# Splitting the output stores of an attention and feed-forward kernel into 32-row pieces

## The chip, the cores and the metric

One core of one Trainium2 chip. The metric is the device time of one execution in microseconds (us); the kernel before takes 597.29 us, the median of three runs (596.9 to 598.46).

## What is computed

Chunked local attention with a few memory keys, and a feed-forward layer on its result. Four sequences of 768 positions, 8 heads of 64; a chunk of 32 queries sees 8 memory keys and a window of 16 + 32 + 8 keys. The heads are put side by side, which gives 3072 tokens of 512 numbers; these go through 512 to 2048 to 512 with a squared, clipped gate. All of it is f32.

```python
for c in range(nc):                       # chunks of 32 queries, 24 a sequence
    k_full = concatenate([mem_k, k_ctx], axis=2)
    v_full = concatenate([mem_v, v_ctx], axis=2)
    scores = scale * matmul(q_c, k_full.transpose(0, 1, 3, 2))
    scores = scores - max(scores, axis=-1, keepdims=True)
    a = exp(scores)
    a = a / (sum(a, axis=-1, keepdims=True) + 1e-09)
    out[:, :, c_start:c_end] = matmul(a, v_full)
x = attn_out.transpose(0, 2, 1, 3).reshape(B * S, H * D)
h = x @ w_in
g = where(h >= 1, h, where(h <= -1, 0, (h + 1) ** 2 / 4))
return g @ w_out
```

## The kernel before, in words

The 3072 tokens are six blocks (`blk` 0 to 5) of 512 tokens, and each block is four token tiles `t` of 128 rows. A tile of the result is 128 rows of 512 f32, 2 KB a row, 256 KB in all. TensorE adds it up in PSUM over 16 slices `fc` of the hidden layer; then DVE or ACT copies it into an SBUF tile `ob`, and a DMA takes it to `out`.

Blocks 0 and 1 go by a hand-written order of steps (`FIRST`, lines 32 to 46). The rest, the end of block 1 and blocks 2 to 5, goes through a planner (class `Plan`, lines 65 to 174). Each step is told to it by `add(engine, took, emit, reads, writes)`: `took` is what the step is supposed to cost in us, and `reads` and `writes` give its dependencies. `due_times` works back from TensorE's steps to the time by which each step is due. `run` then goes through the steps in simulated time, takes for each engine the one that is ready and due first, and so fixes the order of each engine's queue. A step on another engine is ready only some time after the one it needs has ended: 2.0 us where that one is a DMA step on SP (`AFTER`, line 67). What is issued on an engine is kept in that order, and all instructions are recorded on line 191, the line of the helper that does this. Engines wait in order: what stands behind a waiting instruction waits too.

All DMAs are issued from SP. Blocks 2 and 3 make one pair and blocks 4 and 5 another: the first of a pair is worked out straight, the second from differences, with weights that come back from DRAM in units through seven slots (`SLOTS`, line 1129; `load_unit`, tiles named `u_w`, `u_xth`, `u_xtl` in the trace). A slot's next unit is loaded when TensorE has left the slot.

`store(blk, t, key, src)` (lines 1022 to 1053) copies one finished tile to `ob` and adds the DMA step `put`. For `t` = 3 DVE copies the left half and ACT the right. For `blk` under `first` = 2 `put` is one DMA of 128 contiguous rows. From block 2 on the rows of a pair of tiles alternate in DRAM by 32, so that `put` writes four groups of 32 rows, 64 rows apart, in one DMA, whose DRAM side has the shape 4 x 32 x 512:

```python
rows = out[r0 : r0 + HT, :].rearrange("(n b q) d -> b n q d", b=2, q=CHUNK)
sp.dma_start(rows[b], dst())
```

Where `ob` lies decides who waits for a store. For blocks 2 and 4 it is in the tag `f` (two buffers, used later by `tf` and `uc`). For blocks 3 and 5 all four tiles are one SBUF tile under the tag `w_14`. In `tee_ops(1)` (line 1204), between blocks 3 and 4 on one side and 5 on the other, ACT writes the operand `b22` to that same tag (`high("b22", b(1), x32)`, line 1266; `b<-x` in the trace). So this ACT step waits until the four stores of block 3 have landed. ACT's next steps there are the copy `c` (line 1354), which reads a PSUM bank that TensorE then adds on to, and the cast `gh`.

The DMA step that loads a unit is told to the planner as 2.1 or 2.8 us (line 1162), a store as 0.8 us.

Of the kernel before, what the change touches and what calls it, by code (L numbers as in the profile page):

```python
# [17 lines left out]
CHUNK, LEFT, RIGHT = 32, 16, 8  # L18
TB = 512
NCH = TB // CHUNK  # L20
NT = TB // P
# [43 lines left out]
class Plan:  # L65
# [7 lines left out]
    def place(self, key, *tags, bufs=1):  # L73

        waits = self.waits.setdefault(key, set())
        for tag in tags:
            line = self.tenants.setdefault(tag, [])
            if line:
                waits.update(self.touched.get(line[-1], [])[:1])
            if len(line) >= bufs:  # L80
                waits.update(self.touched.get(line[-bufs], ()))
            line.append(key)

    def add(self, engine, took, emit, reads=(), writes=(), soon=False):

        deps = set()
        for keys, writing in ((reads, False), (writes, True)):
            for key in keys:
                base, part = key if isinstance(key, Part) else (key, None)
                deps |= self.waits.get(base, set())  # L90
                state = self.state.setdefault(base, {})
                for name, (writer, readers) in state.items():
                    if part is None or name is None or name == part:
                        deps.update(writer)
                        if writing:
                            deps.update(readers)
        op = Op(engine, took, emit, deps, len(self.ops))
        op.soon = soon
        for x in deps:
            x.then.append(op)  # L100
        for keys, writing in ((reads, False), (writes, True)):
            for key in keys:
                base, part = key if isinstance(key, Part) else (key, None)
                state = self.state[base]
                if writing:
                    if part is None:
                        state.clear()
                    state[part] = ([op], [])
                else:
                    state.setdefault(part, ([], []))[1].append(op)  # L110
                self.touched.setdefault(base, []).append(op)
        self.ops.append(op)
        return op
# [83 lines left out]
def attn_ffn_kernel(ctx: ExitStack, tc: tile.TileContext, first_qk, first_v, qk, vw, w, out):  # L197
    nc = tc.nc
    engines = (nc.tensor, nc.scalar, nc.vector, nc.gpsimd, nc.sync)
    pe, act, dve, pool, sp = (InOrder(tc, e) for e in engines)  # L200
# [7 lines left out]
    NB = qk.shape[0] + 1  # L208
# [20 lines left out]
    HT = TB // 2  # L229
# [77 lines left out]
    first = 2  # L307
# [404 lines left out]
    a, b = n_first["J9"], len(tokens) - 1  # L712
    put = []
# [16 lines left out]
    add, place = plan.add, plan.place  # L730
# [3 lines left out]
    def tile_of(key, make):  # L734
        if key not in tiles:
            tiles[key] = make()
        return tiles[key]
# [11 lines left out]
    def on(engine, took, reads, writes, call, *args, **kwargs):  # L749

        def emit():
            call(*(a() if callable(a) else a for a in args), **kwargs)

        add(engine, took, emit, reads, writes)
# [241 lines left out]
    def out_job(name, outs, fc, w, reads, blk=None):  # L996

        gh, gl = (part_tile(name, which) for which in ("gh", "gl"))
        kinds = [(gh, 0, ("gh", name)), (gh, 1, ("gh", name)), (gl, 0, ("gl", name))]

        def terms(which):
            def get():
                for t, i in which:
                    g, part, _ = kinds[i]
                    yield (
                        outs[t][1](), g()[:, t * P : (t + 1) * P], w(part), fc == 0 and i == 0,
                        fc == NFC - 1 and i == 2,
                    )

            return get  # L1010

        if fc < NFC - 1:
            for i in range(3):
                mm(terms([(t, i) for t in range(NT)]), NT, [kinds[i][2], *reads], [k for k, _ in outs])
                yield
            return
        for t in range(NT):
            mm(terms([(t, i) for i in range(3)]), 3, [("gh", name), ("gl", name), *reads], [outs[t][0]])
            store(blk, t, *outs[t])
            yield  # L1020

    def store(blk, t, key, src):

        apart = blk in (3, NB - 1)
        ob = ("ob", blk, 0 if apart else t // 2)
        if t == 0 or t == 2 and not apart:
            place(ob, *(("w_14",) if apart else ("f",)), bufs=1 if apart else 2)

        def dst():
            if apart:  # L1030
                return tile_of(ob, lambda: const.tile([P, NT, DM], F32, name="ob4", tag="w_14"))[:, t]
            return tile_of(ob, lambda: apool.tile([P, 2, DM], F32, name="ob", tag="f", bufs=2))[:, t % 2]

        if t == NT - 1:
            on("dve", 0.4, [key], [Part(ob, (t, 0))], dve.tensor_copy, lambda: dst()[:, 0:HD], lambda: src()[:, 0:HD])
            on("act", 0.35, [key], [Part(ob, (t, 1))], act.copy, lambda: dst()[:, HD:DM], lambda: src()[:, HD:DM])
        elif t % 2:
            on("act", 0.6, [key], [Part(ob, (t, 0))], act.copy, dst, src)
        else:
            on("dve", 0.7, [key], [Part(ob, (t, 0))], dve.tensor_copy, dst, src)  # L1040

        def put():
            if blk < first:
                r0 = blk * TB + t * P
                sp.dma_start(out[r0 : r0 + P, :], dst())
            else:
                half, b = divmod(t, 2)
                r0 = blk * TB + half * HT
                rows = out[r0 : r0 + HT, :].rearrange("(n b q) d -> b n q d", b=2, q=CHUNK)
                sp.dma_start(rows[b], dst())  # L1050

        add("sp", 0.8, put, [Part(ob, (t, 0)), *([Part(ob, (t, 1))] if t == NT - 1 else [])], [])

    jobs = []

# [28 lines left out]
    for name in ("D2", "D3"):  # L1084
        n = pair_of[name]
# [204 lines left out]
    for u in range(2):  # L1290
# [90 lines left out]
        a, b = hb  # L1381
# [175 lines left out]
```

## Time and profile before

| | us |
|---|---|
| median of three runs | 597.29 |
| the profiled execution's own time | 596.54 |
| its span, from the first to the last instruction | 594.7 |
| TensorE (PE) busy | 559.4 |
| VectorE (DVE) busy | 392.1 |
| ScalarE (ACT) busy | 319.5 |
| GpSimd (POOL) busy | 56.0 |
| DMA queue of SP, share of 16 engines' span | 59.7% |

The profile shows one execution, in us from its first instruction. A line of a timeline has start, duration, engine, operation, output<-input and the number of instructions merged in it; a bracket gives the idle time of the engine before it and what ended that. "SPq" is SP's queue: the duration of a DMA there is the time it takes SP to issue it, not to move the data. A tile's name stands for all its buffers.

### The profile page before, as it was taken

Reading aid. Unit: us, or ns where it says so; the run is one execution under the profiler, and the core shown is the slowest. Engines: PE = TensorE matmul, PEld = TensorE weight load, DVE = VectorE, ACT = ScalarE, POOL = GpSimd, SP = SyncE. Lnnn points to the kernel's source line nnn. Section 1 sums busy time; section 2 is a strip of 40 time slices with the busy share of each in tenths; the row PEclk is TensorE's granted clock in tenths of the full one; section 3 lists DMA queues with packets and bytes.
Section 4 is the critical chain, followed back from the end, with each engine's and each line's share of the span. In section 5 each row is a group of like instructions: output and inputs, shape, how many; then the busy total and the mean of one; then the engine's idle time right before and its main releaser. Section 6 shows DMA issues by size and latency. Waiting matters only on the chain.

```text
span 594.7 us, 12467 instructions
## 1 busy us (share of the span) xinstructions
PE 559.4 (94%) x5268; PEld 457.2 (77%) x5268; DVE 392.1 (66%) x556; ACT 319.5 (54%) x524; POOL 56.0 (9%) x55
## 2 busy tenths in 40 slices
PE   5899999999999999999999999899599999999990
PEld 3788887888887888887878778688488887888880
DVE  4899899737877858688687686658123566664220
ACT  3987666544766667764655664466243544453210
POOL 1010000007679200000000000000000000000000
PEclk9999999999999999999999999999899999999997
DMA  8999969536481846852664976644533546477102
GB/s 318 422 418 424 407 200 393 216 139 253 165 297 75 316 151 241 304 208 93 240 239 142 352 284 255 229 179 141 208 125 128 192 161 224 166 253 265 50 0 71
DMA packets 35352, 132.93 MB, mean 224 GB/s; under 512 B 3296, under 2 KB 5344, under 8 KB 28896
## 3 DMA queue, kind: packets, MB, share of 16 engines
q1 hardware_dynamic: 35296, 132.13, 59.7%
q8 instruction: 41, 0.67, 0.4%
q14 instruction: 15, 0.12, 0.1%
HBM read 102.76 MB, written 29.36 MB: 222 GB/s over the span
## 4 chain that ended last, share of the span: by engine, by line
PE 79%; DVE 6%; ACT 6%; DMA 4%; issue 2%; SPq 1%; ACTq 0%; DVEq 0%
PE ps_h L191 33%; PE a L191 31%; PE ps_o L191 11%; PE ps_x L191 3%; DMA out_dram<-ob 2%; DMA w<-in_w_dram 2%; PE ps_s L191 1%; DVE f L191 1%; ACT gw L191 1%; DVE gl L191 1%; ACT pt L191 1%; ACT pr L191 1%; ACT wr L191 1%; DVE pr L191 1%; DVE wr L191 1%
## 5 line engine op out<-in xcount | busy, mean ns | idle before, releaser
L191 PE MATMUL ps_h<-xth,wr 128*128 128x512 f32 (+1 forms) x384 | 84.2, 357 | 1.3 <-ACT gw L191 0.6
L191 PEld LDWEIGHTS ps_h<-xth,wr 128*128 128x128 f32 x384 | 64.6, 188 | 13.6 <-DVE gw L191 1.1
L191 PE MATMUL ps_o<-wr,gh 128*128 128x512 f32 x256 | 66.0, 393 | 0.2 <-ACT gh L191 0.2
L191 ACT ACTIVATE gw<-gw 128x512 f32<-128x512 f32 (+1 forms) x104 | 62.3, 599 | 3.2
L191 DVE TENSOR_TENSOR gl<-gw,gh 128x512 fp32r<-128x512 f32 (+1 forms) x72 | 51.4, 719 | 9.5 <-ACT gh L191 8.0
L191 ACT CAST gh<-gw 128x512 fp32r<-128x512 f32 (+1 forms) x72 | 40.8, 570 | 29.0 <-DVE gw L191 22.5
L191 PEld LDWEIGHTS ps_o<-wr,gh 128*128 128x128 f32 x256 | 47.0, 188 | 10.0 <-ACT gh L191 0.6
L191 PE MATMUL a<-u_w,gh 128*128 128x512 f32 x180 | 54.1, 391 | 0.0
L191 DVE TENSOR_TENSOR gl<-gq,gh 128x512 fp32r<-128x512 f32 x32 | 21.9, 688 | 40.7 <-PE ps_h L191 24.4
L191 PE MATMUL ps_h<-xtl,wr 128*128 128x512 f32 (+1 forms) x192 | 46.0, 354 | 0.0
L191 PE MATMUL ps_h<-u_w,gh 128*128 128x512 f32 x132 | 41.1, 391 | 2.2 <-issue 2.2
L191 ACT CAST gh<-gq 128x512 fp32r<-128x512 f32 x32 | 19.7, 622 | 41.2 <-PE ps_h L191 25.9
L191 ACT ACTIVATE gw<-gq 128x512 f32<-128x512 f32 x32 | 20.2, 632 | 38.6 <-DVE gq L191 35.7
L191 PEld LDWEIGHTS a<-u_w,gh 128*128 128x128 f32 x180 | 33.6, 188 | 9.5 <-issue 2.4
L191 DVE SCALAR_TENSOR_TENSOR gw<-ps_h,gw 128x512 f32<-128x512 f32 (+1 forms) x48 | 28.4, 593 | 18.7 <-ACT gw L191 18.6
L191 PEld LDWEIGHTS ps_h<-xtl,wr 128*128 128x128 f32 x192 | 32.9, 189 | 5.2
L191 ACT ACTIVATE gw<-ps_h 128x512 f32<-128x512 f32 (+1 forms) x48 | 25.0, 521 | 22.0 <-PE ps_h L191 15.4
L191 PE MATMUL ps_h<-t,u_w 128*128 128x512 f32 x144 | 36.4, 395 | 0.0
L191 PE MATMUL ps_o<-wr,gl 128*128 128x512 f32 x128 | 36.2, 391 | 0.0
L191 PE MATMUL a<-t,u_w 128*128 128x512 f32 x138 | 35.0, 396 | 0.0
L191 PEld LDWEIGHTS ps_h<-t,u_w 128*128 128x128 f32 x144 | 26.6, 188 | 7.0 <-DVE gq L191 1.5
L191 PEld LDWEIGHTS a<-t,u_w 128*128 128x128 f32 x138 | 25.4, 188 | 7.1 <-DVE gq L191 1.8
(145 smaller groups left out, 1024.1 us busy)
## 6 DMA issues: line engine op xcount, KB each, us to landing
u_w<-d_out SPq DMA_DIRECT2D x39, 512.0 KB, 7.1
qk<-in_qk_dram SPq DMA_DIRECT2D x10, 1536.0 KB, 14.2
w<-in_w_dram SPq DMA_DIRECT2D x14, 1024.0 KB, 17.8
u_w<-d_sum SPq DMA_DIRECT2D x12, 1024.0 KB
v<-in_vw_dram SPq DMA_DIRECT2D x10, 1024.0 KB
d_out<-wr SPq DMA_DIRECT2D x16, 512.0 KB, 9.0
out_dram<-ob SPq DMA_DIRECT2D x24, 256.0 KB, 2.0
u_xtl<-d_out SPq DMA_DIRECT2D x9, 512.0 KB, 5.0
```

The costliest lines, as they stand in the source:

```text
L191: return self.tc.keep_in_program_order(getattr(self.engine, name)(*args, **kwargs))
```

## The change

`put` no longer writes a tile of blocks 2 to 5 in one DMA but in four of 32 contiguous rows (64 KB) each, so that 16 DMAs become 64. Those of the very last tile (block 5, `t` = 3) are issued in turn from SP and from ACT, two each. The cost of the step as told to the planner rises from 0.8 to 1.9 us for these blocks. Blocks 0 and 1 stay as they are.

```diff
             else:
                 half, b = divmod(t, 2)
                 r0 = blk * TB + half * HT
-                rows = out[r0 : r0 + HT, :].rearrange("(n b q) d -> b n q d", b=2, q=CHUNK)
-                sp.dma_start(rows[b], dst())
-
-        add("sp", 0.8, put, [Part(ob, (t, 0)), *([Part(ob, (t, 1))] if t == NT - 1 else [])], [])
+                for n in range(4):
+                    r = r0 + (2 * n + b) * CHUNK
+                    by = act if t == NT - 1 and blk == NB - 1 and n % 2 else sp
+                    by.dma_start(out[r : r + CHUNK, :], dst()[n * CHUNK : (n + 1) * CHUNK])
+
+        add("sp", 0.8 if blk < first else 1.9, put, [Part(ob, (t, 0)), *([Part(ob, (t, 1))] if t == NT - 1 else [])], [])
```

## Rows read from the trace of the kernel before

**Rows 1.** The page: the span in 40 slices, each 14.87 us; busy tenths.

```profile
PE   5899999999999999999999999899599999999990
PEclk9999999999999999999999999999899999999997
```

**Rows 2.** Waits of TensorE: us in total, times, longest.

```profile
PE a L191 <- ACT c L191: 7.2, 1, 7.2
...
PE ps_h L191 <- issue: 2.2, 1, 2.2
```

**Rows 3.** SP's waits, whole span: us in total, times, longest.

```profile
SPq L191 <- DMA w<-in_w_dram: 26.6, 16, 2.2
...
SPq L1553 <- DMA out_dram<-ob: 10.7, 1, 10.7
```

**Rows 4.** The chain of waits around 410 to 434: start, us, what.

```profile
410.12 2.73 PE a L191 x12
...
414.31 13.57 DMA out_dram<-ob
...
427.98 1.04 ACT b L191
429.03 0.50 ACT c L191
...
429.57 4.40 PE a L191 x12
```

**Rows 5.** Timeline of ACT, 418 to 430.

```profile
418.95 0.63 ACT L191 ACTIVATE gw<-gw 128x512 f32<-128x512 f32 x1
427.98 1.04 ACT L191 CAST b<-x 128x1024 fp32r<-128x1024 f32 x1 [8.40 <-DMA out_dram<-ob]
428.93 0.58 ACT L191 COPY c<-a 128x512 f32<-128x512 f32 x1
```

**Rows 6.** Stretches: busy us of PE, PEld, DVE, ACT, POOL; granted clock, DMA share, GB/s.

```profile
422.00:424.00 2.00, 0.36 (x2) 0.00 (x0) 0.00 (x0) 0.00 (x0) 0.00 (x0) 1.00 0.82 292
...
426.00:428.00 2.00, 0.00 (x0) 0.00 (x0) 0.00 (x0) 0.02 (x1) 0.00 (x0) 0.50 0.40 162
...
434.00:436.00 2.00, 2.00 (x10) 1.65 (x9) 1.21 (x2) 1.17 (x2) 0.00 (x0) 1.00 0.00 0
```

**Rows 7.** Timeline of SP's queue around block 3's stores, from 410.

```profile
410.20 0.54 SPq L191 DMA_DIRECT2D out_dram<-ob  x1
411.51 0.32 SPq L191 DMA_DIRECT2D u_w<-d_even  x1
411.88 0.78 SPq L191 DMA_DIRECT2D u_w<-d_out  x1
412.75 3.60 SPq L191 DMA_DIRECT2D out_dram<-ob  x3
```

**Rows 8.** Stretches after the last instruction of TensorE, columns as in rows 6.

```profile
584.00:586.00 2.00, 0.00 (x0) 0.00 (x0) 0.00 (x0) 0.00 (x0) 0.00 (x0) 1.00 0.26 101
...
590.00:592.00 2.00, 0.00 (x0) 0.00 (x0) 0.00 (x0) 0.00 (x0) 0.00 (x0) 0.50 0.26 102
```

**Rows 9.** A stretch with unit loads, columns as in rows 6.

```profile
368.00:370.00 2.00, 2.00 (x26) 1.36 (x33) 0.90 (x2) 1.02 (x2) 0.00 (x0) 1.00 1.07 397
```

**Rows 10.** Timeline of the last tiles: copies and stores.

```profile
579.86 3.09 SPq L191 DMA_DIRECT2D out_dram<-ob  x4
...
581.18 0.37 ACT L191 COPY ob<-ps_h 128x256 f32<-128x256 f32 x1 [0.77 <-PE ps_h L191]
581.59 0.42 DVE L191 COPY ob<-ps_h 128x256 f32<-128x256 f32 x1 [0.39 <-ACT ob L191]
```

**Rows 11.** SP's last instructions, and the stores: ns min/median/max, first and last start.

```profile
L1553 SPq EVENT_SEMAPHORE  x7: 17/28/10696, 583.0 to 594.7; - x7
L191 SPq DMA_DIRECT2D out_dram<-ob x24: 332/542/3667, 130.3 to 582.0; - x24
DMA to landing us min/median/max: 2.0/2.0/2.0
```

**Rows 12.** Timeline of SP's queue: several DMAs in a row.

```profile
0.74 1.82 SPq L191 DMA_DIRECT2D qk<-in_first_qk_dram  x4
16.61 18.22 SPq L191 DMA_DIRECT2D w<-in_w_dram  x10
357.57 5.42 SPq L191 DMA_DIRECT2D out_dram<-ob  x3
537.66 0.90 SPq L191 DMA_DIRECT2D u_xth<-d_out  x2
```

**Rows 13.** The page's DMA issues: KB each, median us from issue to landing.

```profile
w<-in_w_dram SPq DMA_DIRECT2D x14, 1024.0 KB, 17.8
```

**Rows 14.** TensorE's use of a unit in slot `xth0`, 540 to 582.

```profile
L191 PE MATMUL a<-u_xth,gh x8: 389/389/389, 570.1 to 574.0; 128*128 128x512 f32 x8
```

## The prediction, made blind

> **What bounds the kernel now.** Start with the slices of the page. TensorE is at nine tenths or more in nearly all of them [rows 1]; it sets the pace, and stores that run beside it cost nothing. So look for the slices in which it isn't busy. Three stand out: the first ones (loads at the start, which the change doesn't touch), the 29th with five tenths (416 to 431 us), in which the granted clock is down to eight tenths too, and the last one. (The 26th, at eight tenths, comes up below.)
>
> Then ask what TensorE waited for. In the view of its waits the largest entry is a single one of 7.2 us, for ACT's copy `c` [rows 2]. The chain of waits tells why `c` was late: it stands behind ACT's cast `b`, and `b` hangs on a DMA of 13.57 us that writes `out` from `ob` [rows 4]. ACT's own timeline says the same: `gw` ends at 419.58, ACT then sits idle 8.40 us until an output store has landed, and only then come `b` and `c` [rows 5]. This is the reuse of the tag `w_14`: `b` overwrites the tile from which block 3's four stores read.
>
> The last slice is the second place. The last copy ends at 582.01 [rows 10]. SP's last store is issued at 582.0, and then SP waits 10.7 us for it [rows 3, 11].
>
> Why are the stores slow? Between 584 and 592, where nothing else runs, the DMA engines are busy 0.26 of the time and move 101 to 102 GB/s [rows 8]. Of 16 engines 0.26 is 4.2. With unit loads in flight the same engines show 1.07 and 397 GB/s [rows 9]. So a store whose DRAM side is 4 x 32 x 512 is moved by about four engines: four tiles of 262 KB are 1.05 MB, which at 102 GB/s is 10.3 us, and that is the wait at the end. The Trainium skill has the rule for it (DMA: Bandwidth & Descriptors, "Why a DMA increments its semaphore by 16 and not by 1"): the number of engines is the largest that divides the outermost counts of both sides, up to 16. Here that makes 4 of 4 and 128, and the trace agrees with 0.26.
>
> **The change part by part.**
>
> *Spreading.* Each new store has 32 rows on both sides, with no outer count of 4. No row shows a 32-row DMA. Its rate lies between 102 GB/s [rows 8] and 397 [rows 9]; I take the upper end, as its shape is like that of the loads (rows outermost) and not like that of the old stores. At 397 GB/s 64 KB take 0.17 us, so the issue on SP becomes what counts.
>
> *Price of an issue.* The shortest store took SP 0.33 us, the median one 0.54 [rows 11]. What matters is the spacing of DMAs that wait for nothing: four in 1.82 us, or 0.455 each [rows 12], and two in 0.90, or 0.45. I take 0.46, with 0.33 and 0.55 as bounds.
>
> *The end.* Tile 0's store can start at 579.86 as now [rows 10]. SP has 4 + 4 + 4 + 2 = 14 issues, and each tile's copy is done before SP gets to it (the last at 582.01; SP reaches tile 3 at 579.86 + 12 x 0.46 = 585.38). The last issue starts at 579.86 + 13 x 0.46 = 585.84. A store of twice the rows at no backlog lands 2.0 us after its issue [rows 11], which gives 587.84. From the end of the long wait (583.0 + 10.7 = 593.7) to the end of the span are 1.0 us [rows 11], so the span ends at 588.84, a gain of 5.86. With 0.33 it is 587.15 (gain 7.55), with 0.55 590.01 (gain 4.69). ACT's two issues start at 582.01 and are done some 3 us before SP's. ACT has nothing behind them; issued from SP they would add 2 x 0.46 = 0.92.
>
> *The stall near 425.* It cost 7.21 us of waiting. Moreover the granted clock, 1.00 (2.4 GHz) as the wait began, was at 0.50 (1.2 GHz) before it ended, and back at 1.00 in 434 to 436 [rows 6]. The twelve matmuls after the wait took 4.40 us, while twelve of the same kind at full clock take 2.73 [rows 4]: another 1.67. Together 8.88.
>
> How much of it goes? In today's order of SP's queue: tile 0 at 410.20, four issues; two unit loads, 0.9 as in rows 12; then twelve issues [rows 7]. The last starts at 410.20 + 0.9 + 15 x 0.46 = 418.0 and lands at 420.0. `b` then takes 0.95 to the start of `c`, and `c` 0.58, so `c` is done by 421.6. TensorE needed it at 429.57 - 7.21 = 422.36. All of the stall goes, with 0.76 to spare; it would start to come back at an issue of 0.51. At 0.55 some 0.6 us remain.
>
> Two things shift this. SP holds back a DMA when too many are under way: ten weight loads in 18.22 us are 1.99 apart [rows 12], each lands 17.8 us after its issue [rows 13], so about nine are in flight (an estimate), and SP's 26.6 us of waits for such loads are this [rows 3]. Nine spacings of 0.46 are 4.1 us, above the 2.0 of a landing, so stores don't hold up stores. But the stores behind the two unit loads may wait for these, by up to 1 us. The other works for the change. The planner lets `b` be ready 2.0 us after the last store's simulated end; four stores at 1.9 instead of 0.8 put that 4.4 us later, so that it is likely to place `c` ahead of `b` on ACT. Then a late `b` holds up only what comes after `c`. I take the full 8.88 and a bound of 7.
>
> *What is queued behind the longer steps.* 48 DMAs more on SP, at 0.46, are 22 us spread over four blocks, but the old stores were long there too: three took 5.42 us [rows 12] and three 3.60 [rows 7], as against 12 x 0.46 = 5.5 now. A unit load behind them is late by 2 us or so at most. The unit in `xth0` that is issued at 537.66 between block 4's stores [rows 12] is first used at 570.1 [rows 14], 32 us later. That cover hides it; without it each us would be a us of TensorE. Copies to `ob` are due up to 1.1 us earlier for the planner and may change places with other ACT or DVE work; I price that at 0 with 2 us either way.
>
> *The wait of 2.2 us for "issue"* [rows 2] has no releaser in the trace. It falls in the 26th slice, some 10 us after block 2's stores; whether they have to do with it can't be told from here: 0 to 2.2 us of gain, and I take 0.
>
> *Sum.* 8.88 + 5.86 = 14.74 on the profiled execution: 596.54 - 14.74 = 581.8 (span 580.0). The median of the runs is 0.75 above that execution, so 597.29 - 14.74 = 582.55; I say 582.5.
>
> **A rule against it.** What the rows show: four loads issued within 1.82 us [rows 12] overlap, and nothing in them says that small DMAs go one at a time. The Trainium skill (SBUF — State Buffer, "The DMA setup-cost knee") says to coalesce, since transfers of 64 KiB reach only some 138 GB/s. By that figure the sixteen last stores would need 16 x 0.475 = 7.6 us (an estimate from that page), and the end would come about 1 us later than in my sum. No row here shows a 64 KB transfer.
>
> **The rivals.**
>
> *Only the end is gained.* The stall stays, because `b` still comes late (the in-flight limit, loads that the planner now puts between the stores, or another ACT wait of the same length that appears in its place). For it: slack is only 0.76 us. Against: `c` can be placed ahead, and a stall of the old length needs stores that land at 428. 597.29 - 5.86 = 591.4.
>
> *The change doesn't spread the stores.* If 32 rows, too, were moved by four engines, 1.05 MB at 102 GB/s stay 10.3 us in both places. Against it: the loads with rows outermost use all engines [rows 9]. 597, no change. By the Trainium skill's rule on engines, named above, 32 and 32 give 16.
>
> *Slower: the price of an issue.* The place is SP's queue, the mechanism that each DMA costs SP much more than 0.46 us. With c per issue the end is at 579.86 + 13c + 3.0, which is later than 594.7 from c = 0.91 on, and TensorE restarts at 410.20 + 0.9 + 15c + 2.0 + 1.6, later than 429.57 from c = 0.99 on. So above some 0.95 the kernel is slower. At 1.81, which is what three stores in 5.42 us come to [rows 12], the end is 11.7 later and the stall 12.3 longer: 621. Against it: those three were issued onto four engines that were backed up, and uncrowded issues take 0.33 to 0.54 [rows 11].
>
> **How the numbers follow.** Forecast (both gains) 0.82; end alone 0.08; no spreading 0.05; slower 0.05. The low end is 0.33 an issue with the "issue" wait gone as well: 597.29 - 8.88 - 7.55 - 2.2 = 578.7. The high end is 0.55, the stall gone to 7 and 2 us of planner's luck: 597.29 - 7 - 4.69 + 2 = 587.6. Range 578.5 to 588. Within 0.3% (about 1.8 us, what a measurement of this kernel can tell) only the second rival falls: faster 0.90, same 0.05, slower 0.05.
>
> **What would show it.** Right: at the end the DMA share well above 0.26 with stores spaced by 0.45 or so, and SP's last wait near 2 us; no wait of TensorE for `c` near 422, the clock at 1.00 through 440, and ACT's `b` without a long wait for `out_dram<-ob`. Wrong: a share of 0.26 beside 32-row stores (no spreading), issues above 0.9 us (price), or TensorE idle for a unit load after 365, 420 or 545 (a queue behind the stores).

## The result, and the profile after

The changed kernel takes 580.0 us, the median of four runs (578.83 to 582.02), beside 597.1 for the kernel before (596.12 to 598.46): a ratio of 0.9716, with a 95% interval of 0.9682 to 0.9749. Some 17 us are gone; the forecast was 14.7 us less, or 582.5 us. (Measured again for the last experiments below, the two kernels are 15.9 us apart.) The profiled execution took 580.32 us, with a span of 578.5.

The page's slices of the changed kernel, 14.46 us each, answer to [rows 1]. The slice of five tenths is gone, and so is the lower clock beside it; only the start and the end are left. (The second digit of the clock, at 14 to 29 us, is lower than before; that lies in the start, which the change doesn't touch.)

```profile
PE   4799999999999999999999999999999999999994
PEclk9899999999999999999999999999999999999998
```

TensorE's waits (us in total, times, longest) answer to [rows 2]. The 7.2 us for `c` are not there any more, and the largest wait is the first load:

```profile
PE ps_s L191 <- DMA qk<-in_first_qk_dram: 6.2, 4, 3.6
...
PE ps_h L191 <- issue: 0.3, 1, 0.3
```

ACT's timeline around the reuse of `w_14` answers to [rows 5]. Before, `b` stood ahead of the first `c` shown here; now it comes one round later, behind the second, and ACT isn't idle ahead of it: its line has no bracket.

```profile
418.39 0.59 ACT L191 COPY c<-a 128x512 f32<-128x512 f32 x1
...
423.83 0.59 ACT L191 COPY c<-a 128x512 f32<-128x512 f32 x1
424.32 1.05 ACT L191 CAST b<-x 128x1024 fp32r<-128x1024 f32 x1
425.26 0.62 ACT L191 CAST gh<-gw 128x512 fp32r<-128x512 f32 x1
```

SP's queue there answers to [rows 7]. The order is another one, too: the planner has put the next unit's two loads between tile 1 and tiles 2 and 3.

```profile
408.92 1.74 SPq L191 DMA_DIRECT2D out_dram<-ob  x4
...
411.73 1.81 SPq L191 DMA_DIRECT2D out_dram<-ob  x4
415.67 0.34 SPq L191 DMA_DIRECT2D u_w<-d_even  x1
416.06 0.43 SPq L191 DMA_DIRECT2D u_w<-d_out  x1
416.59 4.69 SPq L191 DMA_DIRECT2D out_dram<-ob  x8
```

The end answers to [rows 10, 11]. First the timeline of the last stores, then SP's last instructions (ns min/median/max, first and last start), then stretches with the DMA share and GB/s as the last two columns, which answer to [rows 8]:

```profile
569.67 6.61 SPq L191 DMA_DIRECT2D out_dram<-ob  x14
...
571.39 0.42 DVE L191 COPY ob<-ps_h 128x256 f32<-128x256 f32 x1 [0.39 <-ACT ob L191]
571.85 0.93 ACTq L191 DMA_DIRECT2D out_dram<-ob  x2
```

```profile
L1555 SPq EVENT_SEMAPHORE  x7: 17/28/1127, 576.3 to 578.4; - x7
```

```profile
573.00:574.00 1.00, 0.00 (x0) 0.00 (x0) 0.00 (x0) 0.00 (x0) 0.00 (x0) 1.00 0.93 236
574.00:575.00 1.00, 0.00 (x0) 0.00 (x0) 0.00 (x0) 0.00 (x0) 0.00 (x0) 0.79 0.53 129
575.00:576.00 1.00, 0.00 (x0) 0.00 (x0) 0.00 (x0) 0.00 (x0) 0.00 (x0) 0.50 0.58 150
```

SP issues 14 stores in 6.61 us without a pause, waits 1.13 us instead of 10.70, and the DMA engines are busy 0.53 to 0.93 of the time in these stretches instead of 0.26. From the end of the last copy to the end of the span it was 594.7 - 582.01 = 12.69 us and is 578.5 - 571.81 = 6.69: 6.0 us less.

The last copy itself ends 10.20 us earlier (582.01 to 571.81). The wait for `c` and the slow clock behind it make 8.88 of this; the wait for "issue" near 374 has gone from 2.19 to 0.33, another 1.86. That would be 10.74; some 0.5 went the other way, most of it in the first 30 us, where the first weights landed 0.3 us later in this execution, in a part that the change doesn't touch. So the profiled executions differ by 10.2 + 6.0 = 16.2.

### The profile page after: what moved, and what is told of

It reads as the page before. It is cut to its first block, busy times and chain, and to the rows that moved or that the text cites. A ratio compares the mean times of both kernels' runs of the same rounds, so it can differ in the third digit from the quotient of the medians.

```text
span 578.5 us, 12522 instructions
## 1 busy us (share of the span) xinstructions
PE 557.5 (96%) x5268; PEld 456.5 (79%) x5268; DVE 392.3 (68%) x556; ACT 319.5 (55%) x524; POOL 56.2 (10%) x55
## 4 chain that ended last, share of the span: by engine, by line
PE 82%; DVE 7%; ACT 5%; issue 2%; DMA 2%; SPq 1%; DVEq 0%; ACTq 0%
PE ps_h L191 35%; PE a L191 32%; PE ps_o L191 11%; PE ps_x L191 3%; DMA w<-in_w_dram 2%; PE ps_s L191 2%; DVE f L191 1%; DVE gl L191 1%; ACT gw L191 1%; ACT pt L191 1%; ACT wr L191 1%; DVE pr L191 1%; ACT pr L191 1%; DVE wr L191 1%; ACT w L191 1%
```

## The experiments

The theory to test is the prediction's: old stores were moved by four engines only, this held up `b` and the end, and with stores that use all engines SP's issues set the end. The result raised two rivals. The change also told the planner another cost, and the trace shows another order; perhaps that took the stall away, and not the faster stores. And perhaps it is the size of a store that matters, not the outermost count.

**The planner's cost alone, and the stores alone.** First kernel: stores as before.

```diff
-        add("sp", 0.8, put, [...], [])
+        add("sp", 0.8 if blk < first else 1.9, put, [...], [])
```

> The stores stay as before (one DMA of 4 x 32 x 512 a tile); only the planner is told 1.9 instead of 0.8 us. In the changed kernel ACT's b stands one place later, behind the next copy c. Theory A, the spreading took the stall away: the stores still land some 13 us after the last is issued, b still holds ACT up, TensorE still loses most of 7 us, and the time is 594 to 597. Theory B, the planner's new order is enough by itself: c goes ahead of b, TensorE doesn't wait, and the time is 597.1 - 8.9 = 588.2; the end keeps its 10.7 us wait for the last store in either case.

It took 588.17 us (597.70 before, ratio 0.9844, 0.9816 to 0.9872): theory B's number. It is hit in part by luck: 1.5 us of waiting are left, while the wait for "issue" near 374, 2.2 us before, isn't in this trace. ACT's timeline, TensorE's and SP's waits:

```profile
424.05 0.59 ACT L191 COPY c<-a 128x512 f32<-128x512 f32 x1
429.35 1.04 ACT L191 CAST b<-x 128x1024 fp32r<-128x1024 f32 x1 [4.71 <-DMA out_dram<-ob]
430.30 0.61 ACT L191 CAST gh<-gw 128x512 fp32r<-128x512 f32 x1
```

```profile
PE ps_h L191 <- ACT gh L191: 1.5, 1, 1.5
```

```profile
SPq L1553 <- DMA out_dram<-ob: 10.7, 1, 10.7
```

`b` still waits 4.71 us for the slow stores, but now `c` goes ahead of it, and only the cast `gh` comes late, which costs TensorE 1.5 us instead of 7.2 and no clock (1.00 from 420 to 446). `b` has moved by more than the one place that was expected: a whole round of five steps (`c`, `gh`, two `gw`, `c`), 5.4 us of ACT's timeline, now goes ahead of it. SP's queue has changed as well: the stores of tiles 2 and 3 start at 416.77, behind two more unit loads, as in the changed kernel. So the planner's order, with the waiting step behind the urgent one, is nearly enough by itself. The end is as it was.

The second kernel has the four stores and the old cost of 0.8:

```diff
-        add("sp", 0.8 if blk < first else 1.9, put, [...], [])
+        add("sp", 0.8, put, [...], [])
```

> Four stores of 32 rows as in the changed kernel, but the planner is told 0.8 as before, so that b stands ahead of c on ACT. Theory A, the spreading is enough: by the prediction's sum the stores land at 420.0 in times of before, b is done in time, TensorE doesn't wait, and the time is that of the changed kernel, 579 to 582. Theory B, the order is what took the stall away: b waits, and 7 to 9 us come back, 587 to 590.

582.58 us (ratio 0.9746, 0.9717 to 0.9775). `b` stands ahead of `c` as before, and ACT waits little, TensorE hardly:

```profile
411.50 6.82 SPq L191 DMA_DIRECT2D out_dram<-ob  x12
```

```profile
419.72 1.05 ACT L191 CAST b<-x 128x1024 fp32r<-128x1024 f32 x1 [1.65 <-DMA out_dram<-ob]
420.67 0.58 ACT L191 COPY c<-a 128x512 f32<-128x512 f32 x1
```

```profile
PE a L191 <- ACT c L191: 0.4, 1, 0.4
```

So the spreading, too, is nearly enough alone: either half of the change takes away most of the stall, and together they take all of it. The intervals of this kernel and of the whole change overlap; what sets the traces apart here are these 0.4 us. The row of SP also shows where the prediction's sum was tight: twelve stores took 6.82 us, 0.57 each instead of 0.46. The chain of waits of this kernel names the reason: SP waited for the unit load issued just ahead of the stores, at 410.96, before it went on at 416.13. (SP's waits for the two unit loads ahead of these stores were 0.6 and 0.9 us.)

```profile
410.96 5.15 DMA u_w<-d_out
416.11 0.02 issue
416.13 0.31 SPq L191
...
417.90 1.72 DMA out_dram<-ob
```

**One block at a time.** Block 3 alone and block 5 alone in four stores, the others in one (the planner's cost at 0.8):

```diff
-                for n in range(4):
+                if blk in (3,):          # the other kernel: (5,)
+                    for n in range(4):
...
+                else:
+                    sp.dma_start(rows[b], dst())
```

> Only block 3's tiles go out in four stores each; blocks 2, 4 and 5 and the planner's 0.8 stay. If the stall near 422 to 432 hangs on these four tiles alone, 8.9 us go: 588.2, with the wait at the end as before. If other stores have a part in it, less.

> Only block 5's tiles, the last ones, go out in four stores each, all from SP; planner's 0.8. Only the end changes. From SP alone there are 16 issues: 579.86 + 15 x 0.474 + 1.6 + 1.0 = 589.6 against 594.7, so 5.1 us are gained: 592.0. The stall near 422 to 432 stays.

Block 3 alone: 589.31 us (ratio 0.9862, 0.9836 to 0.9888), with 0.6 us left of TensorE's wait for `c`:

```profile
PE a L191 <- ACT c L191: 0.6, 1, 0.6
```

Block 5 alone: 592.16 us (0.9908, 0.9887 to 0.993); SP's sixteen issues start at 580.74 and take 7.40, and the last copy's end is 590.4 - 582.88 = 7.52 us ahead of the end of the span. So the stall hangs on block 3's four tiles and the end on block 5's, and the gains, 8.4 and 5.5 us, lie apart.

> Only block 2's tiles go out in four stores each; the rest, with the planner's 0.8, as before. It asks for the 2.2 us that TensorE waits for nothing visible near 374. If block 2's stores cause it (four engines backed up from 355 to 366), it shrinks as in the changed kernel (0.3) and the time is 1.9 below: 595.2. If it has to do with something else, 2.2 stay and the time is 597.1.

Block 2 alone: 597.83 us beside 597.72 (ratio 0.9992, 0.9978 to 1.0006), no change that can be seen. Its "issue" wait near 374 was 1.1 us. To know how steady this wait is, the kernel before was traced again:

> The kernel before once more, for a second trace: is the wait of 2.2 us for nothing visible near 374 there again? If it belongs to the kernel, 2 us or so at the same matmul; if it is chance, another length.

```profile
PE a L191 <- ACT c L191: 7.2, 1, 7.2
PE ps_h L191 <- issue: 2.0, 1, 2.0
```

2.0 us there, and 1.9 and 2.0 with block 3 or block 5 alone changed. In the nine traces with other stores for block 2, or with the planner's 1.9, it was 1.1 (block 2 alone), 1.7 (the changed kernel with all from SP, below) and under 0.4 in the other seven. So it is about 2 us in all four traces with the old stores and the old order of block 2, and anything from 0 to 1.7 in the others, one of which has the old stores and only the planner's 1.9. The kernel with all from SP differs from the changed one only in the very last tile, and still has 1.7 where two traces of the changed kernel have 0.3 and less: the wait also varies from one execution to the next. What causes it stays open.

**The number of engines.** Two stores of 64 rows a tile: half as many issues as in the change, but the DRAM side has the shape 2 x 32 x 512.

```diff
-                for n in range(4):
-                    r = r0 + (2 * n + b) * CHUNK
+                for n in range(2):
+                    r = r0 + 4 * n * CHUNK
+                    rows = out[r : r + 4 * CHUNK, :].rearrange("(n b q) d -> b n q d", b=2, q=CHUNK)
                     by = act if t == NT - 1 and blk == NB - 1 and n % 2 else sp
-                    by.dma_start(out[r : r + CHUNK, :], dst()[n * CHUNK : (n + 1) * CHUNK])
+                    by.dma_start(rows[b], dst()[2 * n * CHUNK : 2 * (n + 1) * CHUNK])
```

> Two stores of 64 rows a tile, each with a DRAM side of 2 x 32 x 512; planner's 1.9, the second one of the last tile from ACT. If the outermost count sets the number of engines, two engines move each of these: a DMA share near 0.13 and some 51 GB/s at the end, 1.05 MB take 20.6 us, and the end is some 10 us later than before: about 597.1 + 10 - 8.9 = 598, more if b comes late now. If what counts is the size of a store or the rows in it, 128 KB stores are moved at over 200 GB/s, and with half the issues the end is as early as in the changed kernel or earlier: 578 to 581.

616.08 us (ratio 1.0304, 1.0279 to 1.0329), slower by 18 us. Stretches of the end, then ACT's and TensorE's waits:

```profile
602.00:606.00 4.00, 0.00 (x0) 0.00 (x0) 0.00 (x0) 0.00 (x0) 0.00 (x0) 0.50 0.13 51
```

```profile
ACT b L191 <- DMA out_dram<-ob: 14.5, 1, 14.5
```

```profile
PE ps_h L191 <- ACT gh L191: 11.3, 1, 11.3
```

0.13 of 16 engines is two of them, and 51 GB/s is half of the 101 to 102 of the old stores [rows 8]. So 4 x 32 x 512 used four engines, 2 x 32 x 512 uses two, and larger pieces are slower. The time came out higher than expected because `b` now waits 14.5 us, and TensorE 11.3 behind it, even in the planner's better order; the granted clock fell to 0.50 in this wait and was back at 1.00 from 452. The rule of the Trainium skill (DMA: Bandwidth & Descriptors, "Why a DMA increments its semaphore by 16 and not by 1") gives two engines here, and the trace agrees.

**What sets the end.** Eight stores of 16 rows:

```diff
-                for n in range(4):
-                    r = r0 + (2 * n + b) * CHUNK
+                for n in range(8):
+                    h = CHUNK // 2
+                    r = r0 + (2 * (n // 2) + b) * CHUNK + n % 2 * h
...
-                    by.dma_start(out[r : r + CHUNK, :], dst()[n * CHUNK : (n + 1) * CHUNK])
+                    by.dma_start(out[r : r + h, :], dst()[n * h : (n + 1) * h])
```

> Eight stores of 16 rows a tile (32 KB each), half of the last tile's from ACT; planner's 1.9. Rows are outermost, so all engines can take part, but SP has 28 issues at the end instead of 14. If the issue sets the end, the last starts 14 x 0.474 = 6.6 us later than in the changed kernel: 586.6, about the gain at the end lost again. If the data set it, the time is that of the changed kernel, 580.

588.08 us (ratio 0.9828, 0.9809 to 0.9848). SP's row has the same spacing for half the bytes, 13.49 / 28 = 0.48 us, and the engines are at a third:

```profile
570.75 13.49 SPq L191 DMA_DIRECT2D out_dram<-ob  x28
```

```profile
580.00:582.00 2.00, 0.00 (x0) 0.00 (x0) 0.00 (x0) 0.00 (x0) 0.00 (x0) 0.50 0.31 69
```

The last copy ends 13.5 us before the end of the span, 6.8 more than in the changed kernel; 6.6 were expected. So the issue sets the end, at 0.47 to 0.48 us each for 64 KB and for 32 KB. (`b` waited 4.1 us here, TensorE 0.9 for `gh`.)

The last kernels shift issues between SP and ACT, beside the changed kernel on the same chip:

```diff
-                    by = act if t == NT - 1 and blk == NB - 1 and n % 2 else sp
+                    by = sp                                                # all from SP
+                    by = act if blk == NB - 1 and t and n % 2 else sp      # more from ACT
```

> The changed kernel again, beside the next two on the same chip: 580 us, 0.9716 of before.

> The changed kernel, with all four stores of the last tile issued from SP. If SP's issues set the end, two more at 0.474 make it 0.95 us later: 581.0 where the changed kernel has 580.0. If the data or the landing set it, no difference.

> The changed kernel, with every second store of block 5's tiles 1, 2 and 3 from ACT: SP has 10 issues at the end, ACT 6 after its last copy. If issues set the end, SP's last starts at 569.67 + 9 x 0.474 = 573.9 and ACT's at 571.85 + 5 x 0.474 = 574.2 instead of 575.8: 1.6 us earlier, 578.4. If the two queues share what makes an issue long, the gain is under 0.5.

The medians of six runs were 580.87 for the changed kernel (ratio 0.9732, 0.9702 to 0.9761), 581.40 with all from SP (0.9740, 0.9717 to 0.9762) and 579.29 with more from ACT (0.9709, 0.9686 to 0.9732). They lie in the order expected, but the intervals overlap, so the times alone don't settle it. The traces do, for the end: from the last copy to the end of the span it is 578.5 - 571.81 = 6.69 us in the changed kernel, 579.8 - 572.31 = 7.49 with all from SP, and 576.8 - 571.50 = 5.30 with more from ACT. (A second trace of the changed kernel gives 577.8 - 571.27 = 6.53.) The rows of the last:

```profile
569.35 5.21 SPq L191 DMA_DIRECT2D out_dram<-ob  x10
...
570.73 2.77 ACTq L191 DMA_DIRECT2D out_dram<-ob  x6
```

```profile
573.00:574.00 1.00, 0.00 (x0) 0.00 (x0) 0.00 (x0) 0.00 (x0) 0.00 (x0) 0.50 0.95 275
```

```profile
SPq L191 <- DMA out_dram<-ob: 0.7, 1, 0.7
```

While both queues issue, the stores are moved at 275 GB/s; in the changed kernel it was 129 to 150 while SP issued alone. SP's ten issues took 0.52 us each on average, not 0.47, since SP stopped once, 0.7 us, for an earlier store to land; so some of the gain is lost again. This variant is the fastest of the three by its median and by its end; that its whole time beats the changed kernel's is not certain from its runs.

## Why the prediction was right

*Both places.* The two losses were the ones named, and apart from the wait for "issue" nothing else of size: 7.2 us of waiting for `c` with a slow clock behind it, and 10.7 us for the last store. Block 3 alone gave 8.4 of the 8.88 forecast for the first, block 5 alone 5.5 for the second.

*Spreading.* The four engines read out of the share of 0.26 were confirmed by the two of the 64-row stores. The rate taken for the new stores was too high: not 397 GB/s but 275 with two queues (share 0.95). It had no weight, since the issue was the slower of the two.

*Price of an issue.* Taken as 0.46; SP spaced its last 14 stores by 6.61 / 14 = 0.47. SP's last wait, forecast near 2 us, was 1.13. The landing was taken as 2.0 us after the issue, from a store of four times the size ("twice the rows" in the prediction is a slip: the old plain store has 128 rows and the new one 32). It was 1.7 (417.90 and 1.72 in the chain above). The end gained 6.0 where 5.86 were forecast.

*The stall.* It went whole, but for more than one reason. The prediction's first sum, stores landed by 420.0 in times of before, was too early: with `b` in its old place they landed 1.1 us later (419.62, in a kernel whose first store of block 3 is issued at 408.69, 1.51 us earlier than before: 421.1), because SP was held up by a unit load. That is the wait of "up to 1 us" it had set aside. With this, 0.4 us of TensorE's wait would have stayed. The second reason, that the planner would put `c` ahead of `b`, was given as likely and turned out so, and it is nearly enough alone. What the prediction didn't price is what either half does alone: each takes most of the stall away, so the full 8.88 didn't hang on its sum of the landing.

*What is queued behind.* No unit load came late: TensorE has no wait for a unit in the changed kernel. The planner moved two unit loads between block 3's stores, and TensorE lost nothing by it.

*The missing 1.5 us.* The sum was 14.74, the profiled executions differ by 16.2. The wait for "issue", priced at 0 with 2.2 as a bound, was 1.86 shorter in this execution and took the sum nearly to the bound on that side; 0.14 came at the end; about 0.5 was lost elsewhere, mostly at the start. The term that was mis-sized is that wait, and its cause is not known. As it varies between executions of the same order, this part of the gain is in part chance; the second measurement, with 580.87 beside 596.81, has 15.9 us in all.

*The rule against small transfers.* The Trainium skill's 138 GB/s for 64 KiB (SBUF — State Buffer, "The DMA setup-cost knee") is close to what SP alone reached, 129 to 150 GB/s. But two queues reached 275 with the same transfers, so in this kernel it is SP's issues (64 KB in 0.47 us) that held SP alone to such a rate, and no limit of the transfers.

*The rivals.* "Only the end" fell with the trace; "no spreading" with the share; "price of an issue" with 0.47 where 0.95 was its point.

## What to carry to other kernels

Where a small store or load takes long, look at the DMA share in a stretch where it runs alone, in sixteenths: 0.26 is four of the 16 engines, 0.13 two. When so few move it, the outermost count of the DRAM side is the first thing to look at; splitting along that count cost only issues, here 0.47 us each. Count these issues where nothing hides them, at the end of the kernel, and give a second queue its share of them. A slow transfer far from the critical path may still stop an engine that overwrites its source; look at what stands behind that step in the engine's order, since the order that put this step one round later left 1.5 us of a wait of 7.2, and the faster stores alone left 0.4.

## What the runs showed of the hardware

- The number of engines that move a store followed the outermost count of its DRAM side: 51 GB/s and a share of 0.13 for 2 x 32 x 512, 102 GB/s and 0.26 for 4 x 32 x 512. With 32 rows outermost it was up to 275 GB/s and 0.95.
- An issue from SP costs 0.47 to 0.48 us in a row for 64 KB as for 32 KB, so stores of half the size took twice as long in all. From ACT six took 2.77 us, 0.46 each, beside SP's; SP's ten beside them took 5.21 us, of which 0.7 was a wait for an earlier store to land.
- Stores of 32 rows were moved at 275 GB/s with the engines 0.95 busy, where a stretch with unit loads shows 397 at 1.07 [rows 9]; why the same share moves less here is not shown.
- SP held back a store until a unit load issued some DMAs earlier had landed (the load at 410.96, the store at 416.13, with the four stores and the planner's 0.8), and stores behind unit loads were 0.57 to 0.59 us apart (6.82 / 12 and 4.69 / 8).
- The wait of some 2 us of TensorE near 374, for which no releaser is seen, came at the same place in four traces (1.9 to 2.2 us) and under other stores or another order of SP's queue was 0 to 1.7; with the same order up to the last tile it was 0.3 in one trace and 1.7 in another.
